# Alternating score matmuls with matmuls of the second feed-forward product

## The chip, the core and the metric

The kernel runs on one core of a Trainium2 chip. The metric is the device time of one execution in microseconds (us). Three runs of the kernel before the change gave 2177.33, 2177.47 and 2177.63 us, so the median is 2177.47 us. Beside these there is one profiled execution, whose trace every reading here is taken from.

## What is computed

The program is a channel attention followed by a feed-forward layer. For each of four batches, q, k and v are 6080 x 256 matrices. The scores are a product over the 6080 positions, so they are only 256 x 256 per batch; the feed-forward layer has 24320 tokens, 256 features and 2048 hidden units.

```
qn = q / (norm(q, axis=1) + 1e-6);  kn = k / (norm(k, axis=1) + 1e-6)
s  = kn.T @ qn / tau                 # 256 x 256 for each batch
a  = softmax(s, last axis)
x  = (v @ a).reshape(24320, 256)
h  = x @ w_in;  g = max(0.01*h, h);  out = g @ w_out
```

## The kernel before

The attention matrix of a batch is multiplied into w_in once per batch, so the long work is two products per token tile: the first feed-forward product (v with the folded weights) and the second (the activated hidden units with w_out). Both are done in split arithmetic: an operand is written as a high and a low fp32r part, and each product is three matmuls, high-high, low-high and high-low.

**Steps.** A token tile is 1024 tokens (two halves of 512; the last tile of a batch has two halves of 480). For each tile the kernel makes eight steps, one for each pair of 128-wide blocks of hidden units. From the second tile on, a step uses a seven-product scheme for its 2 x 2 blocks. Its PE work stands in this order: `x` (block B11, 3 matmuls), `y` (B21, 3), out(5), first slot, `x` (T2, 3), `z` (T1, 3), out(5), second slot, `x` (T3, 3), out(8), `x` (T4, 3), `z` (B22, 3), and the rest of the out matmuls (6). `x`, `y`, `z` are banks of PSUM. `out(n)` issues the next n of the 24 matmuls of the second product of the step before; these are the `ps_o` matmuls of line 656. All matmuls of both products have 512 columns (480 in the last tile of a batch).

**What reads PSUM within a step.** The hidden values are built up in the one bank `x`, and ScalarE (ACT) copies intermediate states out with `taken` (line 636): h11 after B11, h12 after T2, h22 after T3. The next matmul that adds to `x` has to wait until the copy has ended: T3 waits for the copy of h12, T4 for the copy of h22. VectorE (DVE) then adds `y` or `z` (line 630), ACT applies the leaky ReLU (620) and writes the high part (621), DVE writes the low part (623), and later the `ps_o` matmuls read these `g_split` tiles.

**Score work of the next batch.** While a batch's feed-forward runs, the scores of the next batch are accumulated in the bank `s` (48 chunks of 128 positions). A chunk costs ACT a cast (158) and a square (150), DVE a subtraction (162) and an addition (153), and PE six matmuls of 256 columns (180, `product`): this is the block of six score matmuls. The cast writes a `qk_split` tile, of which there are three buffers, so the cast of a chunk has to wait until the block of the chunk three before it has been multiplied.

**What sets the order.** Every engine executes its instructions in the order in which the program was built. The builder keeps a queue for each engine (`todo`) with a length for each entry; `slot(queue, room)` takes entries out at fixed places of a step, and `in_order` makes each instruction follow the one issued before on its engine. Score blocks wait in the queue `pe`, which has two slots of one entry in a step; ACT's casts and squares are taken at `slot("act", ...)`, up to three of them between the copies of h12 and h22. The first batch's scores, and 12 chunks of the second batch, are computed ahead of this stage without splitting; the change leaves them alone.

Of the kernel before, what the change touches and what calls it, by code (L numbers as in the profile page):

```python
# [31 lines left out]
def channel_attention_ffn(  # L32
# [17 lines left out]
    nc = tc.nc  # L50
# [23 lines left out]
    def bank(tag, bufs=1):  # L74
        return psum.tile([P, TW], F32, name="ps_" + tag, tag=tag, bufs=bufs)

    def temp(dtype=F32, name="temp"):
        return work.tile([P, TW], dtype, name=name, tag="temp", bufs=8)
# [17 lines left out]
    issued = {}  # L96

    @contextmanager
    def in_order(*engines):
        with ExitStack() as stack:  # L100
            for e in engines:
                if e in issued:
                    stack.enter_context(tc.issue_after(issued[e].ins))
            yield
# [5 lines left out]
    class Scores:  # L110
# [52 lines left out]
                out=sp[:, :, 1, :], in0=self.chunk(j), in1=f32(sp[:, :, 0, :]), op=ALU.subtract  # L163
            )

        def product(self, j):
            first, last = j == 0, j == NCHUNK - 1
            sp = self.split.pop(j, None)
            raw = self.chunk(j)
            if first:  # L170
                nc.tensor.matmul(out=self.s, lhsT=zeros, rhs=raw, start=True, stop=False, skip_group_check=True)
            passes = [None] if sp is None else [(0, 0), (0, 1), (1, 0)]
            for n, of in enumerate(passes):
                for h in range(CH):
                    hs, s = slice(h * P, (h + 1) * P), self.s[:, h * C:(h + 1) * C]
                    if of is None:
                        lhsT, rhs = raw[:, 1, hs], raw[:, 0, :]
                    else:
                        lhsT, rhs = sp[:, 1, of[0], hs], sp[:, 0, of[1], :]
                    mm = nc.tensor.matmul(  # L180
                        out=s, lhsT=lhsT, rhs=rhs, start=False, stop=last and n == len(passes) - 1,
                        skip_group_check=True,
                    )
            return mm


# [404 lines left out]
    def block_product(i, p, ps, a, name, first, last):  # L591
        w, sp = w_split[i, p], v_split[i, name]
        n = widths[i % NT]
        with in_order("pe"):
            for k, (x, y) in enumerate(PASSES):
                mm = nc.tensor.matmul(  # L596
                    out=ps[:, 0:n], lhsT=w[:, x, a, :], rhs=sp[:, y, 0:n],
                    start=first and k == 0, stop=k == 2, skip_group_check=True,
                )
        issued["pe"] = mm  # L600
# [31 lines left out]
    def taken(i, ps):  # L632
        n = widths[i % NT]
        h = temp(name="h")
        with in_order("act"):
            issued["act"] = nc.scalar.copy(out=h[:, 0:n], in_=ps[:, 0:n])  # L636
        return h
# [4 lines left out]
    def ffn_out(i, p):  # L642

        b, t = divmod(i, NT)
        n = widths[t]
        f2 = (p // 2) * FPC + p % 2
        f1 = f2 + 2
        if p == 0:
            o_ps[i] = [[bank("o", 4) for _ in range(CH)] for _ in range(2)]
        for name, f, j in (("C11", f1, 0), ("C22", f2, 1), ("C21", f2, 0), ("C12", f1, 1)):  # L650
            sp = g_split.pop((i, p, name))
            early = name in ("C11", "C22")
            for h in range(CH):
                for k, (x, y) in enumerate(((0, 0), (1, 0), (0, 1))):
                    with in_order("pe"):
                        issued["pe"] = nc.tensor.matmul(  # L656
                            out=o_ps[i][j][h][:, 0:n],
                            lhsT=wo[x][:, f, h * P:(h + 1) * P],
                            rhs=sp[:, y, 0:n],
                            start=p == 0 and early and k == 0,  # L660
                            stop=p == NPAIR - 1 and not early and k == 2,
                        )
                    yield
            if p == NPAIR - 1 and not early:
                n0 = b * N + t * TILE + j * n
                for h, copy in enumerate((nc.scalar.copy, nc.vector.tensor_copy)):
                    o = work.tile([P, TW], F32, name="o_sb", bufs=4)
                    copy(out=o[:, 0:n], in_=o_ps[i][j][h][:, 0:n])
                    nc.sync.dma_start(out=outT[h * P:(h + 1) * P, n0:n0 + n], in_=o[:, 0:n])
# [10 lines left out]
    def slot(queue, room):  # L680
        engine = queue.split("_")[0]
        while True:
            entry = next((x for x in todo[queue] if x[3] <= late["tick"]), None)
            if entry is None or entry[0] > room:
                return
            todo[queue].remove(entry)
            room -= entry[0]
            with in_order(engine):
                ins = entry[1]()
            issued[engine] = ins  # L690

    def put(queue, length, fn, then=(), first=False, ready=0):

# [20 lines left out]
    def acc_tile():  # L714
        return work.tile([P, 2, C], F32, name="sq_acc", bufs=1)

    def chunk_work(sc, j, multiply=True):

        if multiply:
            put("act", 0.6, lambda: sc.cast(j), [  # L720
                ("dve", 0.75, lambda: sc.low(j), [("pe_next", 1, lambda: sc.product(j))]),
            ])
        if j == 0:
            sc.acc = [acc_tile()]
            put("act", 0.6, lambda: sc.square(0, sc.acc[0]))
        else:
            sq = temp(name="sq").rearrange("p (x c) -> p x c", x=2)
            put("act", 0.6, lambda: sc.square(j, sq), [("dve", 0.7, lambda: sc.add_square(sq))])
# [75 lines left out]
        for length, fn in reversed(entries) if first else entries:  # L804
            put("dve", length, fn, (), first, late["tick"] + wait)

    v_entries, late = {}, {"tick": 0}

    def v_begin(i):
        v_entries[i] = list(v_parts(i))  # L810
# [43 lines left out]
    for b in range(1, B):  # L854
        w0 = (b - 1) * WPB
        sc = scores[b]
# [20 lines left out]
    sc, nxt = scores[0], scores[1]  # L877
# [91 lines left out]
    def out(n):  # L969

        while n and outs:
            if next(outs[0], outs) is outs:
                outs.pop(0)
            else:
                n -= 1

    for i in range(NTILES):
        for p in range(NPAIR):
            todo["pe"].extend(todo["pe_next"])
            todo["pe_next"].clear()  # L980
            for fn, args in steps.get(i * NPAIR + p, ()):
                fn(*args)
            if i == 0:
                for tag, free, (name, x, y), n in zip("xyzx", " xyz", BLOCKS, (5, 5, 8, 24)):
                    late["tick"] += 1
                    ps = bank(tag)
                    direct_product(p, ps, x, y)
                    slot("act", 1.4 if p else 0.7)
                    out(n)
                    late["bank"] = free  # L990
                    slot("pe_late", 0 if free == " " else 1)
                    leaky(i, p, name, ps, temp(name="h"))
                    late["tick"] += 1
                    slot("act", 1.4)
                    slot("dve", 2.6 if p else 1.5)
                outs.append(ffn_out(i, p))
                continue
            if p:
                w_split.pop((i, p - 1))
            x, y, z = bank("x"), bank("y"), bank("z")  # L1000
            block_product(i, p, x, A11, "B11", True, False)
            h11 = taken(i, x)
            block_product(i, p, y, A12, "B21", True, True)
            slot("act", 0.65)
            add(i, h11, y)
            late["tick"] += 1
            slot("dve", 1.3)
            out(5)
            slot("pe", 1)
            leaky(i, p, "C11", h11, h11)  # L1010
            late["tick"] += 1
            slot("dve", 2.2)
            block_product(i, p, x, S2, "T2", False, False)
            h12 = taken(i, x)
            slot("act", 1.8)
            block_product(i, p, z, S1, "T1", True, False)
            out(5)
            slot("pe", 1)
            block_product(i, p, x, S3, "T3", False, False)
            h22 = taken(i, x)  # L1020
            add(i, h22, z)
            late["tick"] += 1
            slot("dve", 1.3)
            out(8)
            slot("pe_late", 1)
            leaky(i, p, "C22", h22, h22)
            block_product(i, p, x, A22, "T4", False, True)
            block_product(i, p, z, S4, "B22", False, True)
            add(i, h12, z)
            leaky(i, p, "C21", x, temp(name="h"))  # L1030
            slot("act", 0.65)
            late["tick"] += 1
            slot("dve", 0.8)
            leaky(i, p, "C12", h12, h12)
            out(24)
            outs.append(ffn_out(i, p))
# [31 lines left out]
```

## Time and profile before

| what | value |
|---|---|
| median of three runs | 2177.47 us (2177.33 to 2177.63) |
| profiled execution, first to last instruction | 2175.8 us |
| PE (matmul) | 2162.1 us busy, 99% of the span, 9960 matmuls in the trace |
| PEld (weight loads) | 1811.1 us busy, 83% |
| DVE | 1465.1 us busy, 67% |
| ACT | 1478.3 us busy, 68% |
| second product (`ps_o`, line 656) | 4608 matmuls |
| score matmuls on split operands (line 180) | 792, in 132 blocks of six |
| chain that ended last | 95% PE, 3% DVE, 1% ACT, 1% issue |

The span is 1.7 us shorter than the median of the runs: that much lies ahead of the first and behind the last instruction that the profile shows. A matmul's duration in the trace runs from its start to a modelled end, and the next one starts before that end, so what a matmul costs is read from the distance between starts, not from its duration. The weight load of a matmul stands as a row of its own (PEld) and runs while the matmul ahead of it is streaming.

### The profile page before, as it was taken

The page shows a single profiled execution, that of the slowest core. Times are in us where ns is not written, and L with a number is a line of the kernel's source. Part 1 is how long each engine was busy: PE and PEld are TensorE (multiplying, and loading weights), DVE is VectorE, ACT ScalarE, POOL GpSimd, SP SyncE. Part 2 cuts the span into 40 slices and gives each one's busy share as a digit, 9 for nine tenths or more (in the row PEclk, how much of TensorE's full clock was granted, in tenths as well). Part 3 has the DMA queues.
Part 4 walks back from the last instruction along what each step waited for, and adds up shares of the span by engine and source line. Part 5 has one row for each costly group of instructions (what it writes and reads, how often), then busy time and mean ns, then how long its engine had stood idle before and what let it go on. Part 6 is the DMA issues. An engine that isn't in the chain of part 4 may idle for free.

```text
span 2175.8 us, 27271 instructions
## 1 busy us (share of the span) xinstructions
PE 2162.1 (99%) x9960; PEld 1811.1 (83%) x9960; DVE 1465.1 (67%) x2572; ACT 1478.3 (68%) x2564; POOL 3.5 (0%) x11
## 2 busy tenths in 40 slices
PE   9999999999999999999999999999999999999999
PEld 7787888888888888888888888888888888888887
DVE  7887767766767676675776767666677565565554
ACT  6668777766677777776667777777665666666665
POOL 0000000000000000000000000000000000000000
PEclk9999999999999999999999999999999999999999
DMA  9666434335544343443554434344264342333331
GB/s 339 207 206 219 160 124 161 109 135 188 192 168 145 130 162 124 147 142 103 200 192 168 155 121 157 104 160 161 85 220 157 127 139 105 105 139 104 104 121 35
DMA packets 108533, 327.75 MB, mean 151 GB/s; under 512 B 10992, under 2 KB 29296, under 8 KB 108400
## 3 DMA queue, kind: packets, MB, share of 16 engines
q1 hardware_dynamic: 108400, 326.02, 43.8%
q8 instruction: 78, 1.28, 0.3%
q14 instruction: 55, 0.45, 0.1%
HBM read 267.52 MB, written 58.46 MB: 150 GB/s over the span
## 4 chain that ended last, share of the span: by engine, by line
PE 95%; DVE 3%; ACT 1%; issue 1%; DMA 0%; SPq 0%; ACTq 0%
PE ps_o L656 47%; PE ps_x L596 23%; PE ps_z L596 11%; PE ps_y L596 6%; PE ps_s L180 5%; PE ps_s L421 2%; DVE sq_acc L140 1%; PE ps_x L609 1%; PE ps_z L609 0%; PE ps_y L609 0%; DMA qk_raw<-in_k_dram 0%; DVE f_scale L339 0%; DVE g_split L623 0%; DVE f_raw L345 0%; PE ps_y L421 0%
## 5 line engine op out<-in xcount | busy, mean ns | idle before, releaser
L656 PE MATMUL ps_o<-g_split,w_out_split 128*128 128x512 f32 (+1 forms) x4608 | 1162.2, 388 | 0.1
L656 PEld LDWEIGHTS ps_o<-g_split,w_out_split 128*128 128x128 f32 x4608 | 865.0, 188 | 174.3 <-DVE w_out_split L355 0.5
L623 DVE TENSOR_TENSOR g_split<-h,g_split 128x512 fp32r<-128x512 f32 (+1 forms) x768 | 525.3, 684 | 382.7 <-ACT g_split L621 380.8
L596 PE MATMUL ps_x<-v_split,w_split 128*128 128x512 f32 (+1 forms) x2208 | 620.5, 389 | 1.3 <-ACT h L636 1.3
L620 ACT ACTIVATE h<-h 128x512 f32<-128x512 f32 (+1 forms) x552 | 346.7, 628 | 264.8 <-DVE h L630 264.8
L636 ACT COPY h<-ps_x 128x512 f32<-128x512 f32 (+1 forms) x552 | 320.2, 580 | 279.5 <-PE ps_x L596 278.8
L621 ACT CAST g_split<-h 128x512 fp32r<-128x512 f32 (+1 forms) x768 | 473.5, 617 | 24.2
L596 PEld LDWEIGHTS ps_x<-v_split,w_split 128*128 128x128 f32 x2208 | 405.0, 188 | 75.6 <-ACT h L636 3.3
L630 DVE TENSOR_TENSOR h<-ps_z,h 128x512 f32<-128x512 f32 (+1 forms) x368 | 250.9, 682 | 269.3 <-ACT h L636 266.0
L596 PE MATMUL ps_z<-v_split,w_split 128*128 128x512 f32 (+1 forms) x1104 | 309.1, 388 | 0.0
L596 PEld LDWEIGHTS ps_z<-v_split,w_split 128*128 128x128 f32 x1104 | 207.1, 188 | 42.9 <-DVE h L630 0.6
L596 PE MATMUL ps_y<-v_split,w_split 128*128 128x512 f32 (+1 forms) x552 | 154.2, 388 | 0.0
L620 ACT ACTIVATE h<-ps_x 128x512 f32<-128x512 f32 (+1 forms) x200 | 117.6, 588 | 14.1 <-PE ps_x L609 10.6
L630 DVE TENSOR_TENSOR h<-ps_y,h 128x512 f32<-128x512 f32 (+1 forms) x184 | 125.7, 683 | 1.0 <-PE ps_y L596 0.4
L180 PEld LDWEIGHTS ps_s<-qk_split 128*128 128x128 f32 x792 | 112.4, 190 | 11.1 <-issue 1.0
L596 PEld LDWEIGHTS ps_y<-v_split,w_split 128*128 128x128 f32 x552 | 103.4, 188 | 20.9 <-issue 0.5
L180 PE MATMUL ps_s<-qk_split 128*128 128x256 f32 x792 | 116.4, 283 | 0.0
L158 ACT CAST qk_split<-qk_raw 128x512 fp32r<-128x512 f32 x132 | 81.7, 619 | 45.3 <-PE ps_s L180 39.5
L556 DVE TENSOR_TENSOR v_split<-v_raw,v_split 128x512 fp32r<-128x512 f32 (+1 forms) x142 | 97.2, 686 | 4.5
L153 DVE TENSOR_TENSOR sq_acc<-sq_acc,sq 128x512 f32<-128x512 f32 x141 | 96.2, 683 | 0.0
L162 DVE TENSOR_TENSOR qk_split<-qk_raw,qk_split 128x512 fp32r<-128x512 f32 x132 | 90.3, 684 | 4.6 <-ACT qk_split L158 4.6
L150 ACT ACTIVATE sq<-qk_raw 128x512 f32<-128x512 f32 x141 | 88.6, 633 | 0.0
(122 smaller groups left out, 823.9 us busy)
## 6 DMA issues: line engine op xcount, KB each, us to landing
w_split<-w_dram SPq DMA_DIRECT2D x184, 896.0 KB, 4.7
qk_raw<-in_q_dram SPq DMA_DIRECT2D x92, 256.0 KB, 3.3
qk_raw<-in_k_dram SPq DMA_DIRECT2D x92, 256.0 KB, 3.7
v_raw<-in_vT_dram SPq DMA_DIRECT2D x40, 512.0 KB, 4.7
out_dram<-o_sb SPq DMA_DIRECT2D x80, 256.0 KB, 4.2
w_dram<-w_rest SPq DMA_DIRECT2D x32, 512.0 KB, 3.8
win<-win_dram SPq DMA_DIRECT2D x24, 512.0 KB, 4.2
w_dram<-w_first SPq DMA_DIRECT2D x24, 384.0 KB, 3.2
```

The costliest lines, as they stand in the source:

```text
L150: return nc.scalar.activation(out=out, in_=self.chunk(j), func=AF.Square)
L153: return nc.vector.tensor_tensor(out=self.acc[0], in0=self.acc[0], in1=sq, op=ALU.add)
L162: return nc.vector.tensor_tensor(out=sp[:, :, 1, :], in0=self.chunk(j), in1=f32(sp[:, :, 0, :]), op=ALU.subtract)
L180: mm = nc.tensor.matmul(out=s, lhsT=lhsT, rhs=rhs, start=False, stop=last and n == len(passes) - 1, skip_group_check=True,)
L556: last = nc.vector.tensor_tensor(out=sp[:, 1, 0:w], in0=src, in1=f32(sp[:, 0, 0:w]), op=ALU.subtract)
L596: mm = nc.tensor.matmul(out=ps[:, 0:n], lhsT=w[:, x, a, :], rhs=sp[:, y, 0:n], start=first and k == 0, stop=k == 2, skip_group_check=True,)
L620: nc.scalar.activation(out=out[:, 0:n], in_=h[:, 0:n], func=AF.Prelu, alpha=0.01)
L621: issued["act"] = nc.scalar.copy(out=sp[:, 0, 0:n], in_=out[:, 0:n])
L623: issued["dve"] = nc.vector.tensor_tensor(out=sp[:, 1, 0:n], in0=out[:, 0:n], in1=f32(sp[:, 0, 0:n]), op=ALU.subtract)
L630: issued["dve"] = nc.vector.tensor_tensor(out=h[:, 0:n], in0=ps[:, 0:n], in1=h[:, 0:n], op=ALU.add)
L636: issued["act"] = nc.scalar.copy(out=h[:, 0:n], in_=ps[:, 0:n])
L656: issued["pe"] = nc.tensor.matmul(out=o_ps[i][j][h][:, 0:n], lhsT=wo[x][:, f, h * P:(h + 1) * P], rhs=sp[:, y, 0:n], start=p == 0 and earl ...
```

## The change

The generator `product_steps` yields after each of the six matmuls of a score block. A block that is taken at the second slot of a step is not issued there: it is put into a queue `between`, and each `ps_o` matmul of the second product that is issued from then on is followed by one matmul of that block. Since T3 stands between the second slot and out(8), the step's order becomes T3, then one `ps_o` matmul, one score matmul, and so on six times, then two `ps_o` matmuls, then T4. Blocks taken at the first slot stay together.

```
+        def product_steps(self, j):
...
-                    mm = nc.tensor.matmul(
+                    yield nc.tensor.matmul(
                         out=s, lhsT=lhsT, rhs=rhs, start=False, stop=last and n == len(passes) - 1,
...
                     )
                             stop=p == NPAIR - 1 and not early and k == 2,
                         )
+                    score_step()
                     yield
...
+    between = deque()
+
+    def score_product(sc, j):
+        if not late["spread"]:
+            return sc.product(j)
+        between.append(sc.product_steps(j))
+
+    def score_step():
+        while between:
+            with in_order("pe"):
+                mm = next(between[0], None)
+            if mm is not None:
+                issued["pe"] = mm
+                return
+            between.popleft()
...
             out(5)
+            late["spread"] = True
             slot("pe", 1)
+            late["spread"] = False
             block_product(i, p, x, S3, "T3", False, False)
```

In the built programs, 58 of the 132 blocks are taken apart in this way, and 74 stay as they were. The order on PE in one such step, from the matmuls ahead of the second slot on, before:

```order
L596 MATMUL ps_z<-v_split,w_split 128x512 x3
L656 MATMUL ps_o<-g_split,w_out_split 128x512 x5
L180 MATMUL ps_s<-qk_split 128x256 x6
L596 MATMUL ps_x<-v_split,w_split 128x512 x3
L656 MATMUL ps_o<-g_split,w_out_split 128x512 x8
L596 MATMUL ps_x<-v_split,w_split 128x512 x3
```

and with the change (its lines stand three further down in the file), cut behind the fourth pair:

```order
L599 MATMUL ps_z<-v_split,w_split 128x512 x3
L659 MATMUL ps_o<-g_split,w_out_split 128x512 x5
L599 MATMUL ps_x<-v_split,w_split 128x512 x3
L659 MATMUL ps_o<-g_split,w_out_split 128x512
L180 MATMUL ps_s<-qk_split 128x256
L659 MATMUL ps_o<-g_split,w_out_split 128x512
L180 MATMUL ps_s<-qk_split 128x256
L659 MATMUL ps_o<-g_split,w_out_split 128x512
L180 MATMUL ps_s<-qk_split 128x256
L659 MATMUL ps_o<-g_split,w_out_split 128x512
L180 MATMUL ps_s<-qk_split 128x256
```

T3 (the second `ps_x` row) moved ahead of the score block, and the block's last matmul moved behind T3 and six `ps_o` matmuls.

ACT's order is the same in both programs. In the step that begins at 227.2 us of the trace before, it is this from the copy of h12 on, with the semaphores that each row waits for; before:

```order
L636 COPY h_2131<-ps_x_2097 128x512 [waits PE_49]
L150 ACTIVATE sq_2095<-qk_raw_1712 128x512
L158 CAST qk_split_2134<-qk_raw_1808 128x2x256 [waits DMAHW6_49,DMAHW5_49,PE_49]
L150 ACTIVATE sq_2096<-qk_raw_1808 128x512
L636 COPY h_2154<-ps_x_2097 128x512 [waits PE_49]
```

and with the change:

```order
L639 COPY h_2131<-ps_x_2097 128x512 [waits PE_49]
L150 ACTIVATE sq_2095<-qk_raw_1712 128x512
L158 CAST qk_split_2134<-qk_raw_1808 128x2x256 [waits DMAHW6_49,DMAHW5_49,PE_49]
L150 ACTIVATE sq_2096<-qk_raw_1808 128x512
L639 COPY h_2148<-ps_x_2097 128x512
```

No instruction moved. The cast waits on PE for the last matmul of the block that read its buffer, which is the block at this step's second slot; with the change that matmul comes after T3, so the copy of h22 behind the cast no longer needs a wait of its own.

DVE's order is the same too, and on SP, which issues all DMAs, five loads stand one to three places later than before: two of v at one place, and one of k at each of three others, each behind a load of `w_split`.

More of the change, by code (lines that the diff above doesn't have):

```diff
@@ L164, in low @@
             )
-        def product(self, j):
+        def product_steps(self, j):
             first, last = j == 0, j == NCHUNK - 1
@@ L183, in product @@
                     )
+        def product(self, j):
+            *_, mm = self.product_steps(j)
             return mm
@@ L689, in slot @@
                 ins = entry[1]()
-            issued[engine] = ins
+            if ins is not None:
+                issued[engine] = ins
     def put(queue, length, fn, then=(), first=False, ready=0):
@@ L720, in chunk_work @@
             put("act", 0.6, lambda: sc.cast(j), [
-                ("dve", 0.75, lambda: sc.low(j), [("pe_next", 1, lambda: sc.product(j))]),
+                ("dve", 0.75, lambda: sc.low(j), [("pe_next", 1, lambda: score_product(sc, j))]),
             ])
@@ L805, in v_work @@
             put("dve", length, fn, (), first, late["tick"] + wait)
-    v_entries, late = {}, {"tick": 0}
+    v_entries, late = {}, {"tick": 0, "spread": False}
     def v_begin(i):
```

## The prediction

> **What bounds the kernel now.** I read the page's busy shares first, then the groups of instructions on PE, then the time that whole steps take.
>
> ```profile
> span 2175.8 us, 27271 instructions
> PE 2162.1 (99%) x9960; PEld 1811.1 (83%) x9960; DVE 1465.1 (67%) x2572; ACT 1478.3 (68%) x2564; POOL 3.5 (0%) x11
> PEclk9999999999999999999999999999999999999999
> PE 95%; DVE 3%; ACT 1%; issue 1%; DMA 0%; SPq 0%; ACTq 0%
> L656 PE MATMUL ps_o<-g_split,w_out_split 128*128 128x512 f32 (+1 forms) x4608 | 1162.2, 388 | 0.1
> L180 PE MATMUL ps_s<-qk_split 128*128 128x256 f32 x792 | 116.4, 283 | 0.0
> ```
>
> PE is busy all through and its clock is full throughout; the chain that ended last is PE for 95%. So time goes away only if PE's matmuls stand closer together, and any new wait on PE is added in full, since no idle time is there to take it up. What a score block costs is read from whole steps, as stretches of the span from one step's first matmul to the next one's:
>
> ```profile
> 1414.82:1425.02 10.20, 10.20 (x47) 8.45 (x45) 8.56 (x15) 7.95 (x15) 0.00 (x0) 1.00 0.81 278
> 308.36:319.30 10.94, 10.94 (x53) 9.17 (x51) 8.23 (x14) 7.63 (x14) 0.00 (x0) 1.00 0.56 183
> 250.54:261.64 11.10, 11.10 (x53) 9.09 (x51) 8.74 (x15) 8.24 (x15) 0.00 (x0) 1.00 0.72 261
> 238.86:250.54 11.68, 11.68 (x59) 9.88 (x57) 9.29 (x17) 8.54 (x16) 0.00 (x0) 1.00 0.24 78
> ```
>
> The first column is the step's length. A step without a score block takes 10.20 us for 45 matmuls of 512 columns, 0.2267 each. One block adds 0.74, two add 1.48. If 256 columns took half of 0.2267, six would take 0.68. A block thus costs 0.06 us more than its columns, and 58 blocks 3.5 us: **this is all that the change can win**, 0.16% of the time. The third row is a step with one block that lost another 0.16; it returns below.
>
> Next comes one step with both slots taken, PE and ACT side by side, and the single-block step of 250.54 where it stalled:
>
> ```profile
> 229.67 0.88 PE L180 MATMUL ps_s<-qk_split 128*128 128x256 f32 x6
> 230.38 0.86 PE L596 MATMUL ps_x<-v_split,w_split 128*128 128x512 f32 x3
> 230.59 0.62 ACT L158 CAST qk_split<-qk_raw 128x512 fp32r<-128x512 f32 x1 [1.94 <-PE ps_s L180]
> 231.11 0.63 ACT L620 ACTIVATE h<-h 128x512 f32<-128x512 f32 x1
> 231.77 0.62 ACT L621 CAST g_split<-h 128x512 fp32r<-128x512 f32 x1
> 232.30 0.58 ACT L636 COPY h<-ps_x 128x512 f32<-128x512 f32 x1
> 232.91 0.88 PE L180 MATMUL ps_s<-qk_split 128*128 128x256 f32 x6
> 233.62 0.86 PE L596 MATMUL ps_x<-v_split,w_split 128*128 128x512 f32 x3
> 233.82 0.62 ACT L158 CAST qk_split<-qk_raw 128x512 fp32r<-128x512 f32 x1 [0.41 <-PE ps_s L180]
> 234.32 1.99 PE L656 MATMUL ps_o<-g_split,w_out_split 128*128 128x512 f32 x8
> 234.34 0.63 ACT L150 ACTIVATE sq<-qk_raw 128x512 f32<-128x512 f32 x1
> 234.88 0.56 ACT L636 COPY h<-ps_x 128x512 f32<-128x512 f32 x1
> 236.14 0.84 PE L596 MATMUL ps_x<-v_split,w_split 128*128 128x512 f32 x3
> ...
> 255.66 0.58 ACT L636 COPY h<-ps_x 128x512 f32<-128x512 f32 x1
> 256.29 0.53 PEld L596 LDWEIGHTS ps_x<-v_split,w_split 128*128 128x128 f32 x3 [0.29 <-ACT h L636]
> 256.29 0.96 PE L596 MATMUL ps_x<-v_split,w_split 128*128 128x512 f32 x3
> ```
>
> Two things are to be seen. The cast at 230.59 waited 1.94 us for the first slot's block and pushed the copy of h12 behind it to 232.30–232.88, 0.03 us ahead of the second slot's block; the block itself then hides that the copy came late. And the cast at 233.82 waited for the last matmul of the second slot's block; the copy of h22 (234.88) stands behind it, and T4 (236.14) waits for that copy.
>
> **The change part by part.** It adds and removes no matmul, cast or copy. It moves the second slot's block in 58 steps, and three things follow.
>
> *1. The distance between matmuls.* No row shows 256 and 512 columns in alternation, so this is bounded. From below: all of the 0.06 goes, −0.06 us per block. The nearest row for that is a block's first matmul, the one score matmul whose own load ran under 512 columns:
>
> ```profile
> 229.78 0.76 PE L180 MATMUL ps_s<-qk_split 128*128 128x256 f32 x5
> ```
>
> The listing that begins behind the first matmul has the second at 229.78, 0.11 behind 229.67; the other five take 0.60 until 230.38, 0.12 each. From above: a T3 behind a block takes 0.70 (233.62 to 234.32) where 3 x 0.2267 is 0.68. If all six score matmuls took 0.12 and each of the six returns to 512 columns cost 0.01, half of that, a block would cost 0.72 + 0.06 = 0.78 instead of 0.74, +0.04. I take −0.02, a third of the gain, since both rows bear on the pattern and the first is the nearer one. In the 48 steps without a larger wait this is −1.0 us (−2.9 to +1.9).
>
> The Trainium skill, "TensorE: Matmul & The Clock Gate", section on LDWEIGHTS, gives a weight load as columns divided by 1.2, which for 128 columns is 107 ns. By that a load would fit under 256 columns everywhere and this part would be 0 instead of −1.0 us; the first distance of 0.11 agrees with it, the other five of 0.12 do not.
>
> *2. T3 loses its cover.* T3 now stands where the block stood, and its weight load has to be issued one matmul earlier still, at 232.68 in the step shown. Where the copy of h12 ended early, nothing happens: in 35 of the 58 steps it ended 1.0 us ahead of the block, as in the first of them below (209.99 against 211.03). In 23 steps, from the one shown to the last row below (1487.64 against 1487.66), it ended 0.03 us ahead:
>
> ```profile
> 209.40 0.59 ACT L636 COPY h<-ps_x 128x512 f32<-128x512 f32 x1 [0.46 <-PE ps_x L596]
> 211.03 0.88 PE L180 MATMUL ps_s<-qk_split 128*128 128x256 f32 x6
> 218.34 0.62 ACT L158 CAST qk_split<-qk_raw 128x512 fp32r<-128x512 f32 x1
> ...
> 1487.06 0.58 ACT L636 COPY h<-ps_x 128x512 f32<-128x512 f32 x1
> ```
>
> The price is in the trace: at 255.66 the same late copy met a T3 without a block. The load began 0.05 behind the copy's end (256.24), T3's three matmuls took 0.11 longer (0.96 against 0.84 to 0.86), and the step took 11.10 instead of 10.94. I take 0.15 us, between the 0.14 of start and stretch and the 0.16 of the step. For the 13 of these 23 steps that part 3 doesn't contain: +1.95 us (1.8 to 2.1).
>
> The same page of the Trainium skill, in the section on the array's architectural detail, lets PE's queue pull weight loads ahead of matmuls in flight. If it did so across this wait, 0.11 of each 0.15 would go, 2.5 us in 23 steps; the row at 256.29 shows the load itself waiting for ACT.
>
> *3. A cast that waits for the spread block holds ACT.* Waits of casts for score blocks are these:
>
> ```profile
> L158 ACT CAST qk_split<-qk_raw x132: 606/622/627, 196.7 to 1506.7; 128x512 fp32r<-128x512 f32 x132
>   PE ps_s L180: 39.5, 31
>   DMA w_split<-w_dram: 5.8, 3
> ...
> 235.47 0.69 DVE L630 TENSOR_TENSOR h<-ps_z,h 128x512 f32<-128x512 f32 x1 [1.76 <-ACT h L636]
> 242.26 0.62 ACT L158 CAST qk_split<-qk_raw 128x512 fp32r<-128x512 f32 x1 [1.65 <-PE ps_s L180]
> ...
> 1431.66 0.62 ACT L158 CAST qk_split<-qk_raw 128x512 fp32r<-128x512 f32 x1 [0.41 <-PE ps_s L180]
> ```
>
> The three put down to a DMA are 1.93 us each like the row at 230.59 and belong to the others: 34 in all. In ACT's rows ten of them are of the 0.41 kind, the first at 233.82, the last at 1431.66; these wait for the block of their own step's second slot. The other 24 wait for a first slot's block (45.3 − 10 x 0.41 = 41.2, 1.7 each), which doesn't move.
>
> For the ten, in the times of the step shown: T3 starts at 232.93 with the stall of part 2, so the first `ps_o` matmul at 232.91 + 0.14 + 0.68 = 233.73. The sixth score matmul starts after six `ps_o` distances and five score distances: 233.73 + 6 x 0.227 + 5 x (0.113 to 0.123) = 235.66 to 235.71. It ends 0.28 later (mean 283 ns above), and the cast starts 0.04 behind that (before: the last one started at 233.50, ended at 233.78, and the cast came at 233.82): 235.98 to 236.03, a shift of 2.16 to 2.21. Square and copy follow as before, so the copy of h22 ends at 235.44 + 2.16 to 2.21 = 237.60 to 237.65. T4 starts 0.05 later and its first matmul takes 0.11 longer, against 236.14: **1.62 to 1.67 us lost per step**, part 2's stall included. Ten times 1.65 is +16.5 us.
>
> Behind this wait stand, on PE, T4, then B22 into `z`, which needs DVE's add of h22 and `z`; that add begins 0.03 behind the copy and takes 0.69 (235.47), so it ends 0.72 behind it, while B22's first matmul is due 0.84 behind it (0.05 and T4's stretched 0.79): its load waits a little, and I allow 0.02 us. ACT is 2.16 behind where PE is 1.65 behind; in all ten the next first-slot cast idles about 1.65 us for PE (the one at 242.26 here), which takes up the 0.5. If that cover were gone, 0.5 us more per step would be lost.
>
> *What costs nothing.* The q and k loads on SP that move one to three rows are asked for some three steps ahead, over 30 us, and land in 4:
>
> ```profile
> qk_raw<-in_k_dram SPq DMA_DIRECT2D x92, 256.0 KB, 3.7
> v_raw<-in_vT_dram SPq DMA_DIRECT2D x40, 512.0 KB, 4.7
> ```
>
> If one of the five did come late, it would hold ACT or DVE by at most its 3.7 or 4.7 us once. In the other 48 steps the third cast behind a spread block starts 6.4 us or more after the block's end (211.91 and 218.34 above), which covers the 2.2; without that cover they would be as dear as the ten. The last blocks of a batch have a step or more until the softmax reads them.
>
> **Sum.** −1.0 + 1.95 + 16.5 = +17.5 us on the profiled 2175.8 us. The 1.7 us around the span in the median run stay, so 2177.47 + 17.5 = 2195.0 us. Its own range goes by the bounds: 2177.5 − 2.9 + 1.8 + 16.2 = 2192.6 to 2177.5 + 1.9 + 2.1 + 17 = 2198.5 (17: ten times 1.67 with the 0.02 behind it).
>
> **The rivals.**
>
> *A: the waits are hidden and the closer matmuls remain* (3.5 us at most: 2174 us; with the part-1 value 2176 to 2177). It holds if ACT's casts need not wait for the spread block. For it: ACT is busy 68% only. Against it: the order shows the cast waiting for PE ahead of the copy of h22, and 0.41 us of waiting is already in the trace where the block ends 2.2 us earlier. Chance 8%; only its extreme could count as faster.
>
> *B: only part 3 is half as large*, because the delayed ACT work of a step is partly done in PE's first stalls and T4 is met with less: 8 instead of 16.5, 2186 us. For it: ACT catches up 1.65 in a step. Against: nothing stands between the cast and the copy of h22 but one square. Chance 7%.
>
> *C: ACT's lag is carried on.* The 0.5 us by which ACT falls behind PE reaches the next step's copy of h11 and T2: +0.5 x 10, 2200 us. For it: in the step shown every later ACT instruction of the step follows the copy of h22. Against: the 1.65 idle ahead of the next first-slot cast. Chance 10%.
>
> *D: alternating is dear*: each return to 512 columns costs the whole 0.02 us that T3 loses behind a block now. Then a spread block takes 0.72 + 0.12 = 0.84 instead of 0.74, and 48 of them add 4.8 us where I put −1.0: 2201 us. It would decide if a spread step without waits took 11.78. Chance 5%.
>
> **How the numbers follow.** The forecast has 70%. About 0.2%, 4.4 us, is what a measurement of this kernel tells from no change. The forecast, B, C and D are slower: 92%, of which I leave 2 to smaller stalls than any of these; the same: 7%, A's main part and those; faster: 3%, since even the whole gain of part 1 stays below 4.4. The range of 2188 to 2201 us holds the forecast's own range, the upper end of B, C, and half of D.
>
> **What would show it.** In the changed trace: ten casts at line 158 that waited about 2.6 us instead of 0.41 for PE; PE idle for ACT ahead of ten T4, 1.5 us each, and a short stall ahead of 23 T3; those ten steps 13.3 us long, the 13 others about 11.8, the 35 without late copies at 11.66. The prediction is wrong if the ten T4 start without a wait, if steps with early copies differ from 11.68 by more than 0.06, or if step lengths elsewhere change.

## The result and the profile after

The change made the kernel slower: 2198.25 us median (2197.9 to 2199.8) against 2177.51 us (2177.33 to 2177.63), 20.7 us more. The ratio is 1.0095, with a 95% interval of 1.0083 to 1.0106. The forecast was 2195.0 us, with a range of 2188 to 2201 us.

The lines of the changed kernel's page that answer to those shown before (its lines stand three further down, so 599, 659 and 639 are what 596, 656 and 636 were):

```profile
span 2197.9 us, 27277 instructions
PE 2171.3 (99%) x9960; PEld 1807.0 (82%) x9960; DVE 1470.2 (67%) x2572; ACT 1485.7 (68%) x2564; POOL 3.5 (0%) x11
L659 PE MATMUL ps_o<-g_split,w_out_split 128*128 128x512 f32 (+1 forms) x4608 | 1205.1, 388 | 0.1
L599 PE MATMUL ps_x<-v_split,w_split 128*128 128x512 f32 (+1 forms) x2208 | 623.6, 390 | 13.7 <-ACT h L639 13.7
L180 PE MATMUL ps_s<-qk_split 128*128 128x256 f32 x792 | 163.2, 282 | 0.0
```

PE's share still reads 99%, and yet the `ps_x` matmuls now have 13.7 us of idle time ahead of them that ACT ended, where it was 1.3. The busy time of the `ps_o` and `ps_s` groups grew although a single matmul lasts as long as before: in the alternation the two groups overlap in time, and each counts the overlap. So the groups' busy times do not show where the time went. The waits and the step lengths do. From the table of waits after the change (the columns are us in total, times, longest), with those of the kernel before behind it:

```profile
ACT qk_split L158 <- PE ps_s L180: 56.9, 31, 2.6
PEld ps_x L599 <- ACT h L639: 26.7, 39, 1.7
PE ps_x L599 <- ACT h L639: 13.7, 11, 1.3
```

```profile
ACT qk_split L158 <- PE ps_s L180: 39.5, 31, 1.9
PEld ps_x L596 <- ACT h L636: 3.3, 6, 1.7
PE ps_x L596 <- ACT h L636: 1.3, 1, 1.3
```

Weight loads waited for ACT's copy 39 times instead of 6, which is 33 more: 23 T3 and 10 T4. Matmuls were idle for it 11 times instead of once: the ten T4. The casts wait as often as before, but 17.4 us longer.

The lengths of whole steps after the change, one of each kind (the first column is the length):

```profile
206.97:218.67 11.70, 11.70 (x58) 9.87 (x57) 8.50 (x14) 8.86 (x16) 0.00 (x0) 1.00 0.37 126
228.87:242.27 13.40, 12.15 (x58) 9.64 (x57) 6.21 (x11) 7.97 (x15) 0.00 (x0) 1.00 0.32 108
293.57:305.43 11.86, 11.86 (x59) 9.79 (x58) 8.56 (x14) 8.29 (x15) 0.00 (x0) 1.00 0.36 120
317.12:328.06 10.94, 10.94 (x52) 9.16 (x51) 8.18 (x14) 7.61 (x14) 0.00 (x0) 1.00 0.52 180
```

A step with two blocks was 11.68. Steps whose second block alternates and meets no wait are 11.70 now (33 steps; two more, which carry two further matmuls, went from 12.54 to 12.56), those with a late copy of h12 11.85 to 11.87, and the ten with a waiting cast 13.40 to 13.45. The last row, a step with one block at the first slot, is as before. Adding up: 10 x 1.74 + 13 x 0.175 + 35 x 0.02 = 17.4 + 2.3 + 0.7 = 20.4 us, against 20.7 between the medians. (The profiled execution of the change is 1.5 us longer than the median of its runs would let one expect; its first split score block, ahead of which the change moves nothing, starts at 209.47 us where it started at 207.79.)

The step at 228.87 is the one that the prediction worked through. Its rows after the change:

```profile
233.99 0.58 ACT L639 COPY h<-ps_x 128x512 f32<-128x512 f32 x1
234.62 0.53 PEld L599 LDWEIGHTS ps_x<-v_split,w_split 128*128 128x128 f32 x3 [0.29 <-ACT h L639]
234.62 0.96 PE L599 MATMUL ps_x<-v_split,w_split 128*128 128x512 f32 x3
235.43 0.39 PE L659 MATMUL ps_o<-g_split,w_out_split 128*128 128x512 f32 x1
235.66 0.28 PE L180 MATMUL ps_s<-qk_split 128*128 128x256 f32 x1
...
237.39 0.28 PE L180 MATMUL ps_s<-qk_split 128*128 128x256 f32 x1
237.51 0.63 PE L659 MATMUL ps_o<-g_split,w_out_split 128*128 128x512 f32 x2
237.71 0.62 ACT L158 CAST qk_split<-qk_raw 128x512 fp32r<-128x512 f32 x1 [2.61 <-PE ps_s L180]
238.24 0.62 ACT L150 ACTIVATE sq<-qk_raw 128x512 f32<-128x512 f32 x1
238.77 0.56 ACT L639 COPY h<-ps_x 128x512 f32<-128x512 f32 x1
239.38 0.53 PEld L599 LDWEIGHTS ps_x<-v_split,w_split 128*128 128x128 f32 x3 [1.68 <-ACT h L639]
239.38 0.97 PE L599 MATMUL ps_x<-v_split,w_split 128*128 128x512 f32 x3 [1.25 <-ACT h L639]
240.11 0.54 PEld L599 LDWEIGHTS ps_z<-v_split,w_split 128*128 128x128 f32 x3 [0.19 <-DVE h L633]
```

T3's load waits for a copy that ends at 234.57; the sixth score matmul starts at 237.39; the cast, which had waited 0.41 us before, now waits 2.61; one square and then the copy of h22 follow, and T4 begins 0.05 us after that copy has ended at 239.33. PE is busy with the two last `ps_o` matmuls until 238.13 and idle for the 1.25 us up to T4.

### The profile page after: what moved, and what is told of

Same layout as the page of the kernel before. It is cut to its first block, busy times and chain, and to the rows that moved or that the text cites. A ratio compares the mean times of both kernels' runs of the same rounds, so it can differ in the third digit from the quotient of the medians.

```text
span 2197.9 us, 27277 instructions
## 1 busy us (share of the span) xinstructions
PE 2171.3 (99%) x9960; PEld 1807.0 (82%) x9960; DVE 1470.2 (67%) x2572; ACT 1485.7 (68%) x2564; POOL 3.5 (0%) x11
## 4 chain that ended last, share of the span: by engine, by line
PE 95%; DVE 2%; ACT 1%; DMA 1%; issue 0%; SPq 0%; ACTq 0%
PE ps_o L659 46%; PE ps_x L599 23%; PE ps_z L599 11%; PE ps_y L599 6%; PE ps_s L180 5%; PE ps_s L424 2%; PE ps_x L612 1%; DVE sq_acc L140 1%; DMA qk_raw<-in_k_dram 1%; PE ps_z L612 0%; PE ps_y L612 0%; ACT qk_split L158 0%; ACT h L639 0%; ACT sq L150 0%; DVE g_split L626 0%
## 5 line engine op out<-in xcount | busy, mean ns | idle before, releaser
L659 PE MATMUL ps_o<-g_split,w_out_split 128*128 128x512 f32 (+1 forms) x4608 | 1205.1, 388 | 0.1
L599 PE MATMUL ps_x<-v_split,w_split 128*128 128x512 f32 (+1 forms) x2208 | 623.6, 390 | 13.7 <-ACT h L639 13.7
L180 PE MATMUL ps_s<-qk_split 128*128 128x256 f32 x792 | 163.2, 282 | 0.0
L180 PEld LDWEIGHTS ps_s<-qk_split 128*128 128x128 f32 x792 | 128.6, 189 | 9.0 <-issue 1.0
```

Source lines behind the costliest of these rows:

```text
L180: yield nc.tensor.matmul(out=s, lhsT=lhsT, rhs=rhs, start=False, stop=last and n == len(passes) - 1, skip_group_check=True,)
L599: mm = nc.tensor.matmul(out=ps[:, 0:n], lhsT=w[:, x, a, :], rhs=sp[:, y, 0:n], start=first and k == 0, stop=k == 2, skip_group_check=True,)
L659: issued["pe"] = nc.tensor.matmul(out=o_ps[i][j][h][:, 0:n], lhsT=wo[x][:, f, h * P:(h + 1) * P], rhs=sp[:, y, 0:n], start=p == 0 and earl ...
```

## Experiments

Two theories were set against each other first. The one of the prediction: the loss sits in waits on ACT, in 23 steps that the order of ACT's work picks out. The rival: alternating 512 and 256 columns is dear in itself, and every taken-apart block pays its share. In the edits below, a block's number counts the 132 score blocks in the order in which they stand on PE.

**The ten kept together.**

```
 def score_product(sc, j):
-    if not late["spread"]:
+    block = j + (-12, 36, 84)[sc.b - 1]
+    if not late["spread"] or block in (3, 5, 8, 10, 21, 23, 53, 70, 101, 118):
         return sc.product(j)
```

> The ten blocks whose own step has a cast waiting for them stay together at the second slot; the other 48 alternate as in the change. If the loss sits in waits on ACT (1.73 us in each of ten steps, 0.17 in 13 others, 0.02 in 35 by the changed kernel's step lengths), 13 x 0.17 + 35 x 0.02 = 2.9 us remain over the kernel before: 2180.4 us. If alternating costs the same in every step (20.7 us over 58 blocks, 0.36 each), 48 of them keep 17.1 us: 2194.6 us.

Measured: 2181.04 us against 2177.82, ratio 1.0015 (1.0006 to 1.0025). Of the 20.7 us, 17.5 went with ten blocks of 58; 3.2 remain, where 2.9 were expected from the waits and 17.1 from an even cost. The weight loads that still wait are the 6 of the kernel before and the 13 T3:

```profile
PEld ps_x L599 <- ACT h L639: 7.0, 19, 1.7
```

**The ten alone.** The same edit with `not in`.

> Only the ten blocks whose own step has a cast waiting for them alternate; the other 48 stay together. Waits: 10 x 1.73 = 17.3 us over the kernel before, 2194.8 us, with ten steps of 13.4 us. Evenly spread cost: 3.6 us, 2181.1 us.

Measured: 2195.58 us, ratio 1.0082 (1.0067 to 1.0097), which is 17.8 us over 2177.82. From its waits:

```profile
PEld ps_x L599 <- ACT h L639: 23.0, 26, 1.7
PE ps_x L599 <- ACT h L639: 13.7, 11, 1.3
```

26 waits of weight loads are 6 plus the ten T3 and the ten T4. Ten blocks alone make most of the loss, and the two runs together make the whole of it (3.2 + 17.8 = 21.0), so these parts add up.

**All 23 with late copies kept together.** The same edit with the numbers of the 23 blocks.

> All 23 blocks in steps where the copy of h12 comes late stay together; the 35 others alternate. Waits: only the distance between matmuls is left, 35 x 0.02 = 0.7 us over the kernel before, 2178.2 us; part 1 of the prediction (-0.02 a block) gives 2176.8 us. Evenly spread cost: 12.5 us, 2190.0 us.

Measured: 2178.6 us against 2177.82, ratio 1.0005 (0.9995 to 1.0014). The ratio alone cannot tell 35 x 0.02 = 0.7 us from nothing, but its steps with an alternating block are 11.70 us long in the profile, and the waits of weight loads on ACT are back where they were:

```profile
PEld ps_x L599 <- ACT h L639: 3.3, 6, 1.7
```

So 35 taken-apart blocks without a wait cost 0.02 us each, and win nothing.

**Four buffers for the split scores.** This takes away what makes the casts wait and leaves all 58 blocks taken apart. (The cut leaves out three more places at which the same tiles are declared and 3 becomes 4.)

```
-            sp = work.tile([P, 2, 2, C], F32R, name="qk_split", bufs=3)
+            sp = work.tile([P, 2, 2, C], F32R, name="qk_split", bufs=4)
...
-        return work.tile([P, TW], dtype, name=name, tag="temp", bufs=8)
+        return work.tile([P, TW], dtype, name=name, tag="temp", bufs=6)
```

> The change with four qk_split buffers instead of three; to make room the temporaries of ACT and DVE have six buffers instead of eight. The order on every engine is the same. Waits: a cast then waits for the block four before its own, which is never in its own step, so ACT is not held, neither T3 nor T4 waits, and 58 x 0.02 = 1.2 us remain: 2178.7 us. Evenly spread cost: unchanged at 2198.2 us. If six temporaries are too few, new waits of ACT or DVE on temporaries show, and the time is in between.

Measured: 2178.77 us against 2177.82, ratio 1.0002 (0.9992 to 1.0012). No cast is listed as waiting for anything, and no T3 or T4 of a spread step waits:

```profile
L158 ACT CAST qk_split<-qk_raw x132: 606/621/626, 196.8 to 1507.8; 128x512 fp32r<-128x512 f32 x132
PEld ps_x L599 <- ACT h L639: 3.0, 5, 1.7
```

The five loads that still wait do so in the kernel before too. Of the 58 steps with a taken-apart block, 56 are 11.70 us long and the two with further matmuls 12.56. With the same order on PE, almost all of the loss is gone: it came from the waits, and the waits from the three buffers.

**The same buffers without the change.** The two edits above, in the kernel before.

> The kernel before with the same four qk_split buffers and six temporaries as in the run of the change with four buffers; the order on every engine is that of the kernel before. Waits: the casts' 34 waits are gone here too, but PE did not wait for them except in the one step of 11.10, so 0.16 us faster at most: 2177.3 us, and the change with four buffers stays about 1.2 us slower than this. If the six temporaries cost something, this is slower than the kernel before by as much.

Measured: 2177.53 us against 2177.69, ratio 0.9999 (0.999 to 1.0008). Six temporaries cost nothing, and the casts' waits cost the kernel before next to nothing, since PE met them only in the step of 11.10, which is 10.94 here. The two kernels with four buffers are 1.24 us apart by their medians, and 1.1 if each is measured from the kernel before of its own series; the intervals of both hold 1, so the times alone do not secure it. The step lengths do: 11.70 against 11.68 in 56 steps, 12.56 against 12.54 in two, 58 x 0.02 = 1.2 us. That is the alternation alone.

**T3 covered again.** In the steps with a taken-apart block T3 stands behind the third pair.

```
             late["spread"] = False
+            ahead = 3 if between else 0
+            out(ahead)
             block_product(i, p, x, S3, "T3", False, False)
...
-            out(8)
+            out(8 - ahead)
```

> The change, but in the 58 steps with a taken-apart block T3 stands behind the third pair instead of ahead of the first; the order on ACT and DVE is the change's. Waits: T3 has 1.0 us of cover again, so the 13 steps of 11.85 go back to about 11.70 (-0.15 each, 2.0 us in all); in the ten others the last score matmul still ends behind six ps_o matmuls and T3, only the 0.15 of T3's own stall goes, and about 1.58 of 1.73 stays: 2198.2 - 2.0 - 1.5 = 2194.7 us. If losing T3's cover were what makes the ten steps dear, they would fall below 12 and the time to about 2179 us.

Measured: 2194.92 us against 2177.69, ratio 1.0078 (1.0064 to 1.0092). From its steps, one of the ten and one of the thirteen:

```profile
227.36:240.62 13.26, 12.01 (x58) 9.72 (x57) 6.20 (x11) 7.94 (x15) 0.00 (x0) 1.00 0.34 111
291.52:303.23 11.71, 11.71 (x59) 9.87 (x58) 8.10 (x14) 7.81 (x15) 0.00 (x0) 1.00 0.36 122
```

The thirteen fell from 11.86 to 11.70 or 11.71, the ten only from 13.40 to 13.45 down to 13.27 to 13.33. So T3's lost cover is worth 0.13 to 0.15 us wherever the copy of h12 is late, 0.02 is the alternation, and the rest of the ten steps' loss is the cast.

**What the alternation costs: pairs and triples.** Part 1 of the prediction had the wrong sign, so the way in which the score matmuls are mixed was varied in the 35 steps without waits: `score_step` issues two (or three) of them behind a `ps_o` matmul before it returns.

```
+        taken_now = 0
         while between:
...
                 issued["pe"] = mm
-                return
-            between.popleft()
+                taken_now += 1
+                if taken_now == 2:
+                    return
+            else:
+                between.popleft()
```

> As the run in which the 23 blocks of steps with a late copy stay together, but the 35 others go out as two score matmuls behind each of three ps_o matmuls instead of one behind each of six. If every return to 512 columns costs a fixed amount, three returns cost less than six and more than one: steps between 11.68 and 11.70 us. If the alternation costs by the number of score matmuls that follow 512 columns directly (0.113 against 0.120 at a block's first matmul), pairs are worse than singles: over 11.70.

Measured: 2179.37 us against 2177.69, ratio 1.0009 (0.9999 to 1.0018). The time fits a step that is 0.05 longer in 35 steps, 1.6 us. The one execution of this kernel whose trace was kept took 9445 us, so the step lengths come from a repeat, and three in a row were run beside it:

> The same kernel as the run with two score matmuls behind each of three ps_o matmuls, for the step lengths at the chip's full clock. Twelve score matmuls in a row cost 1.46 us, six 0.74, which is 0.12 each and 0.02 for the return; six single ones cost 0.76, which is 0.0067 for each return. If a return costs 0.02 after any run of two or more, pairs cost 0.72 + 3 x 0.02 = 0.78 and the step 11.72 us; if it grows with the run's length from 0.0067, they cost 0.72 + 3 x 0.0133 = 0.76 and the step stays at 11.70.

> Three score matmuls behind each of two ps_o matmuls in the same 35 steps. If a return costs 0.02 after any run of two or more: 0.72 + 2 x 0.02 = 0.76, a step of 11.70 us; if it grows with the run's length up to 0.02: 0.76 at three too, so triples tell the two apart only together with the pairs. If the clock's grid and not the number of returns decides, neither holds.

Measured, one execution each: 2179.49 and 2178.24 us, against 2177.28. The step with pairs and the one with triples:

```profile
205.41:217.13 11.72, 11.72 (x58) 9.88 (x57) 8.49 (x14) 8.85 (x16) 0.00 (x0) 1.00 0.35 125
```

```profile
205.43:217.12 11.69, 11.69 (x59) 9.88 (x58) 8.51 (x14) 8.86 (x16) 0.00 (x0) 1.00 0.34 123
```

A second block thus makes the step 11.68 as one run of six, 11.69 as two of three, 11.73 as three of two (the mean of 33 such steps; the row's ends are cut to hundredths) and 11.70 as six single matmuls. A fixed 0.02 for each return fits six, three and two about (11.68, 11.70, 11.72), but not the singles, for which it gives 11.78. Neither a fixed price nor one that grows with the run's length fits all four. Pairs are worse than singles, as the second reading ahead of the first run expected, but a cost by the number of score matmuls that follow 512 columns directly would make triples and the whole run worse still, and they are better.

**Both blocks at the first slot.** If mixing costs, keeping more together should win. In the kernel before:

```
             out(5)
-            slot("pe", 1)
+            slot("pe", 2)
             leaky(i, p, "C11", h11, h11)
```

> The kernel before with room for two score blocks at the first slot, so that 47 steps have twelve score matmuls in a row there and none at the second slot. If a block pays once for its start and its end, twelve in a row cost 0.113 + 11 x 0.12 and the one return, 1.46 us instead of 2 x 0.74: 0.02 saved in 47 steps, 0.9 us, 2176.6 us. T3 starts as long after the first slot's block as before, so the late copies of h12 cost nothing, and the casts that waited 0.41 us for the second slot's block no longer wait. Rival: T2 follows 0.7 us later and holds the copy of h12 and T3: slower than before.

Measured: 2176.44 us against 2177.69, ratio 0.9994 (0.9985 to 1.0003): 1.2 us less, where 0.9 were expected, but the interval holds 1. (In 14 of the 47 steps the edit does not empty the second slot: a third block stands there.) The profile tells more, with a step of two blocks and one of three:

```profile
207.17:218.83 11.66, 11.66 (x58) 9.88 (x57) 8.32 (x14) 8.66 (x16) 0.00 (x0) 1.00 0.35 124
229.03:241.43 12.40, 12.40 (x64) 10.60 (x63) 7.03 (x12) 8.57 (x16) 0.00 (x0) 1.00 0.35 116
```

Twelve in a row take 1.46 us instead of 1.48, in all 47 steps. That makes the 0.9, and the one step of 11.10 us, which is gone, makes another 0.16. T2, which comes 0.7 us later, held nothing up. This version has the lowest median of all the kernels run: clearly below the change, and below the kernel before by an amount that its interval does not secure.

## Why the prediction held, and where it was off

**What bounds the kernel** held: PE had no idle time to give, and every wait that the change put on it appears in full in a step's length, 0.175 us in thirteen steps and 1.74 in ten, the alternation's 0.02 included.

**Part 1, the distance between matmuls, had the wrong sign.** It took −0.02 us for a block and −1.0 in all; it is +0.02, by the 35 steps without a wait and by the 58 steps of the two kernels with four buffers. It lies inside the stated bounds of −0.06 to +0.04. The step that failed is the choice between two rows: the prediction took the first distance of a block, 0.11 us, as the nearest row for a single score matmul, and gave the other row, the price of a return to 512 columns, too little weight. In a step without a wait, the one at 206.97, three of the six pairs read:

```profile
213.95 0.28 PE L180 MATMUL ps_s<-qk_split 128*128 128x256 f32 x1
214.07 0.40 PE L659 MATMUL ps_o<-g_split,w_out_split 128*128 128x512 f32 x1
214.31 0.28 PE L180 MATMUL ps_s<-qk_split 128*128 128x256 f32 x1
214.43 0.40 PE L659 MATMUL ps_o<-g_split,w_out_split 128*128 128x512 f32 x1
214.66 0.28 PE L180 MATMUL ps_s<-qk_split 128*128 128x256 f32 x1
214.78 0.40 PE L659 MATMUL ps_o<-g_split,w_out_split 128*128 128x512 f32 x1
```

Averaged over the 33 such steps of 11.70 us, the next `ps_o` matmul starts 0.113 us behind the first and the fourth score matmul, but 0.118 behind the second and the fifth and 0.120 behind the third and the sixth; and each `ps_o` matmul behind a score matmul takes 0.236 until the next start instead of 0.227, which is the 0.01 of the upper bound. So the alternation saves 0.01 us on the score matmuls (0.703 instead of 0.712 for six) and pays 0.06 at its returns, where one run of six pays 0.03. By the rule of the Trainium skill that the prediction quotes ("TensorE: Matmul & The Clock Gate", section on LDWEIGHTS) this part would be 0, which is nearer than the forecast; the runs show +0.02, which the rule does not give.

**Part 2, T3's lost cover, held.** 33 waits more in the profile are the 23 T3 and the ten T4; a T3 stall was put at 0.15 us, and the thirteen steps lost 0.175, of which 0.155 remains when the alternation's 0.02 is taken off. Covering T3 again gave 0.15 back. The stretch of T3's three matmuls is there in full (0.96 us in the rows above), and their load waited for ACT too, so no load was pulled ahead across this wait.

**Part 3, the cast that holds ACT, held in its place and its count, and was 5% too small**: 1.74 us for a step instead of 1.65 (PE's idle time ahead of T4 is 1.25 us of it, where 1.5 had been named as the sign). In the step worked through, T4 starts 1.54 us later within the step than before, inside the 1.51 to 1.56 foreseen. Behind it T4 and B22 lose 0.17 instead of the 0.13 allowed: T4's three matmuls last 0.97 instead of 0.84, and B22's load waits 0.19 for DVE. Of the whole gap of 3.2 us between 2195.0 and 2198.25, part 1 makes 1.9 (48 x 0.04), part 3 0.9 (10 x 0.09) and part 2 0.1; 0.3 is left over.

**The rivals.** A (waits hidden) and B (part 3 half as large) are out by the ten steps of 13.40 and by the run of the ten alone. C (ACT's lag carried on) is out, by the cover that was named for it, and the steps behind the ten have their usual lengths. The first-slot cast of the next step, which had idled 1.65 us at 242.26, idles 1.17 now:

```profile
245.68 0.62 ACT L158 CAST qk_split<-qk_raw 128x512 fp32r<-128x512 f32 x1 [1.17 <-PE ps_s L180]
```

That takes up the 0.5, and it is why the casts' waits grew by 17.4 us and not by 10 x 2.2. D (alternating is dear) would have needed steps of 11.78; they are 11.70.

## What to carry to other kernels

Before a block of matmuls is moved later in order to mix it with others, look at who waits for its last matmul, and at what stands behind that waiter on its engine: here a cast, two places ahead of the copy that PE needs next, turned 2.2 us of later block into a step 1.7 us longer, in ten steps of 184. A block that seems to cost something may also be hiding something: T3 lost its cover where a copy ended only 0.03 us ahead. And what the finer mix can win is bounded beforehand from step lengths (0.06 us a block here), which tells whether any new wait is affordable.

## What the runs showed of the hardware that was not expected

Matmuls of 256 and 512 columns do not simply add up by their columns. By step lengths, six score matmuls in one run cost 0.74 us, twelve 1.46, two runs of three 0.75, six single ones 0.76 and three pairs 0.79, where the columns alone give 0.68 for six and 1.36 for twelve. The trace shows where the pairs lose: the ten matmuls of 512 columns behind the last pair, on through T4 into B22, stand 0.233 us apart on average instead of 0.227, where behind the last of six singles only the first one does (0.236). Why this is so was not settled; no run took the weight loads and the widths apart.
